# Block-sparse attention and a softplus layer on one core: the transposed probabilities written by one 128-row transpose and 16 copies by DMA instead of 16 small transposes

## The chip, the cores and the metric

The kernel runs on one core of one Trainium2 chip. The metric is device time in microseconds (us) of one launch, lower is better. Engines are named as in the profile: PE (TensorE matmul), PEld (its weight loads), DVE (VectorE), ACT (ScalarE), POOL (GpSimd), and SP (SyncE), which here only issues DMAs. Each engine runs its own queue in order and waits on semaphores.

## The reference, cut to what matters

```python
# q, k, v: (8, 8, 576, 64); heads 0..3 local, heads 4..7 strided, stride 32
scores = scale * np.matmul(q, k.transpose(0, 1, 3, 2))
rel = pos[:, None] - pos[None, :]
mask_local = (rel >= 0) & (rel < 32)
mask_strided = (rel >= 0) & (pos[None, :] % 32 == pos[:, None] % 32)
attn = softmax(np.where(mask, scores, -1e9))
x = np.matmul(attn, v)            # -> (4608, 512)
h = x @ w_in                      # (4608, 2048)
g = np.maximum(h, 0.0) + np.log1p(np.exp(-np.abs(h)))
out = g @ w_out                   # (4608, 512), float32
```

## The kernel before

**Attention.** The eight heads of a batch are handled as four pairs, so there are 32 pairs, numbered n = 0 to 31. A query sees at most 32 keys, so a block of 32 queries needs only 64 keys. For one pair the scores are a tile of 128 rows (two places times two heads times 32 queries) by 9 chunks of 64 keys. `head_scores` (L402 on PE) makes them, `add_mask` (L461), `row_maxima` (L466), `row_subtract` (L470), `row_exp` (ACT), `row_sums` (L493), `reciprocals` (L501) and `normalize` (L505) turn them into probabilities on DVE, in a tile of 128 by 576.

**Transposes.** The product with v needs the probabilities with keys in the partitions: a tile `pt` of 128 keys, for two heads, six key tiles `a` and three query blocks `i` of 32. Query block `i` has values only in the partition quarters `i` and `i + 1`; the other quarters stay zero. `prob_transposes` (L516) writes it straight: 16 transposes of 32 rows for a pair, eight of 192 columns and eight of 96, each moving its 32-row blocks to the quarter where they belong. In the planner they are four tasks of four instructions, `P{n}.0` to `P{n}`. `weighted` (L584 on PE) then multiplies with v. Except for a few pairs PE does the scores of pair n and the product of pair n - 1 in one stretch (`work` in `scores_of`); the text calls this the joint stretch.

**The layer.** The 4608 tokens are nine chunks of 512. `hidden` (L718) multiplies by w_in, `log_part` and `softplus` (L742) follow, `g_high` and `g_low` (L772) split the result in two parts, and `output` (L787) multiplies by w_out. Each product is three float32r products of high and low parts. The last four chunks are done two and two: seven products (`product`, L890) serve two chunks, with the sums of x and w made beforehand. One turn of that loop (a lap) has the products 1, 2, 5, 6, 3, 7, 4. The results are kept in four half tiles, `kept_0` and `kept_1`: ACT copies the bank of product 6 to the second half of `kept_1` (L981), product 7 then adds to the same bank, DVE joins product 3 to `kept_1` (L986), softplus writes the value back there, and SP stores it to DRAM as `far_u` (L748). The next lap's copy of product 6 may overwrite that half only when the store has landed.

**Order.** The first part of the program follows a list of names written out by hand (`FIRST`), up to pair 7. All later work is placed by `Plan`: each task has an urgency, an engine, a cost, what it waits for, and a lateness after its end for DMAs. The planner gives each task the first gap on its engine that is long enough, and the program's order on every engine is that of the planned start times. The planned times decide the order alone; on the chip each engine waits for what it really needs.

**DMA.** All DMAs of this part are issued by SP. They take eight semaphores in turn, so a DMA's issue also waits until the DMA eight places ahead has landed. A pair's q is loaded into the buffer of its probabilities (L284), its k into one of two buffers `kT` (L309), and v into one buffer (L320, L327). Weights w_in that no longer fit are streamed (L701), and in the laps SP loads `ws` (L969), `near` (L972) and `away` (L975).

The lines that fix the waits around the change:

```python
add(f"Y{n}{j}", y + j, "DVE", 0.47, fn, [f"S{n}", f"P{n-2}"])   # mask of pair n: its buffer is free
s2_free = [f"{spent}.{f-1}"] if f else s1_free                   # spent is the store of far_u
task("k2", "ACT", 0.6, fn, [f"P6.{A}.{f}", *s2_free])            # copy of product 6
mul("7", [f"k2.{A}.{f}"] + ([] if f else [...]))                 # product 7 adds to the same bank
```

## Time and profile before

| | |
|---|---|
| median of 3 runs | 864.98 us (863.56 to 865.66) |
| profiled execution, its own time | 865.16 us |
| its span (first to last instruction) | 863.1 us |
| granted PE clock | 1.0 throughout |
| ACT busy | 492.2 us (57%) |
| DMA: packets, bytes | 74477 packets, 119.49 MB, mean 138 GB/s |

The time of a run is some 2 us more than the span, for what lies around the first and last instruction. A busy share says little by itself: an engine may be busy all the time and still not set the end, and an engine with 74% may hold up another in one place. So the stretches and the waits are read, not the shares alone.

In the timeline a row has the start in us from the span's start, the time of the group, the engine, the line of the kernel, the operation with its tiles, and how many instructions were merged. A bracket at the end tells how long the engine was idle before it and what ended that. `SPq` rows are DMA issues: the time that SP spends on issuing, not the transfer.

### The profile page before, as it was taken

How to read it: one execution, taken by the hardware profiler on the slowest of the kernel's cores; microseconds unless marked ns; L12 is line 12 of the kernel's file. 1: busy time of each engine (PE TensorE's matmuls, PEld its weight loads, DVE VectorE, ACT ScalarE, POOL GpSimd, SP SyncE). 2: the span in 40 equal slices, each digit the busy share in tenths (PEclk: the TensorE clock that was granted, in tenths of full speed). 3: DMA queues.
4: the chain of work that ended last, by engine and by line, in shares of the span. 5: the costliest groups of instructions: out<-in, count | busy, mean ns of one | idle time of the engine just before them, and what ended most of it. 6: DMA issues, size and time to landing. Idle time of an engine off the chain costs nothing.

```text
span 863.1 us, 16559 instructions
## 1 busy us (share of the span) xinstructions
PE 853.4 (99%) x6536; PEld 700.7 (81%) x6536; DVE 640.9 (74%) x1370; ACT 492.2 (57%) x913; POOL 65.9 (8%) x88
## 2 busy tenths in 40 slices
PE   7999999999999999999999999999999999999998
PEld 6787888888888888888888888888888888888886
DVE  7899977898798879888788976677687746656500
ACT  6898755655555555546555555766664355566400
POOL 6345550000000000000000000000000000000000
PEclk9999999999999999999999999999999999999999
DMA  9794114646313453135424433655546143333100
GB/s 330 284 348 155 55 42 152 205 148 218 119 46 99 132 185 106 58 107 164 126 86 145 142 106 118 202 176 169 175 147 197 50 158 134 111 124 120 47 27 24
DMA packets 74477, 119.49 MB, mean 138 GB/s; under 512 B 5664, under 2 KB 41632, under 8 KB 74400
## 3 DMA queue, kind: packets, MB, share of 16 engines
q1 hardware_dynamic: 74112, 118.12, 41.4%
q8 instruction: 51, 0.84, 0.4%
q10 hardware_dynamic: 288, 0.33, 0.1%
q14 instruction: 26, 0.21, 0.1%
HBM read 88.01 MB, written 30.41 MB: 137 GB/s over the span
## 4 chain that ended last, share of the span: by engine, by line
PE 92%; DVE 4%; ACT 2%; issue 1%; DMA 0%; POOL 0%; ACTq 0%; POOLq 0%
PE py L787 43%; PE ph L718 23%; PE bank_a L890 10%; PE bank_c L890 5%; PE bank_b L890 2%; PE pv L584 2%; PE ps L402 2%; PE po L584 2%; PE py_last L787 1%; PE po L402 1%; PE pt L554 1%; DVE home L516 1%; DVE a_i L672 0%; DVE a_o L672 0%; DMA raw_q<-in_qk_dram 0%
## 5 line engine op out<-in xcount | busy, mean ns | idle before, releaser
L787 PE MATMUL py<-w_o,gh 128*128 128x512 f32 x1024 | 318.5, 392 | 0.0
L787 PEld LDWEIGHTS py<-w_o,gh 128*128 128x128 f32 x1024 | 190.3, 188 | 41.4 <-DVE o L287 0.3
L718 PE MATMUL ph<-x_h,w_i 128*128 128x512 f32 x656 | 202.8, 390 | 0.5 <-DVE u L742 0.5
L787 PE MATMUL py<-w_o,gl 128*128 128x512 f32 x512 | 199.3, 389 | 0.0
L516 DVE STREAM_TRANSPOSE home<-home 32x192 f32<-32x192 f32 x448 | 140.7, 318 | 7.1
L718 PEld LDWEIGHTS ph<-x_h,w_i 128*128 128x128 f32 x656 | 122.6, 188 | 26.7 <-POOL home L505 0.9
L718 PE MATMUL ph<-x_l,w_i 128*128 128x512 f32 x328 | 127.7, 389 | 0.0
L287 ACT CAST gh<-u 128x512 fp32r<-128x512 f32 x89 | 55.2, 621 | 107.7 <-DVE u L742 84.7
L787 PEld LDWEIGHTS py<-w_o,gl 128*128 128x128 f32 x512 | 96.1, 188 | 20.3
L730 ACT ACTIVATE u<-ph 128x512 f32<-128x512 f32 x84 | 50.1, 598 | 90.8 <-PE ph L718 88.2
L772 DVE TENSOR_TENSOR gl<-u,gh 128x512 fp32r<-128x512 f32 x117 | 80.8, 691 | 19.3 <-ACT gh L287 15.7
L735 ACT ACTIVATE u<-u 128x512 f32<-128x512 f32 x144 | 90.9, 632 | 3.8
L733 ACT ACTIVATE u<-u 128x512 f32<-128x512 f32 x144 | 90.9, 632 | 3.6
L718 PEld LDWEIGHTS ph<-x_l,w_i 128*128 128x128 f32 x328 | 61.6, 188 | 13.0
L742 DVE SCALAR_TENSOR_TENSOR u<-ph,u 128x512 f32<-128x512 f32 x84 | 57.7, 687 | 13.7 <-ACT u L735 12.5
L730 ACT ACTIVATE u<-kept 128x512 f32<-128x512 f32 x45 | 28.4, 631 | 41.1 <-DVE kept L986 25.6
L287 DVE COPY o<-py 128x512 f32<-128x512 f32 (+1 forms) x15 | 10.0, 669 | 45.6 <-PE py L787 45.5
L986 DVE TENSOR_TENSOR kept<-bank_c,kept 128x512 f32<-128x512 f32 x15 | 10.4, 692 | 33.8 <-PE bank_c L890 33.8
L287 ACT COPY home<-home 128x576 f32<-128x576 f32 x26 | 33.4, 1284 | 1.7 <-DMA home<-in_qk_dram 1.7
L287 ACT COPY o<-py 128x512 f32<-128x512 f32 (+1 forms) x21 | 11.5, 574 | 38.4 <-PE py L787 27.6
L461 DVE TENSOR_TENSOR home<-ps,home 128x384 f32<-128x384 f32 x28 | 15.5, 554 | 23.5 <-PE ps L402 22.0
L981 ACT COPY kept<-bank_a 128x512 f32<-128x512 f32 x30 | 17.6, 586 | 25.8 <-PE bank_a L890 24.2
(197 smaller groups left out, 1188.7 us busy)
## 6 DMA issues: line engine op xcount, KB each, us to landing
home<-in_qk_dram SPq DMA_DIRECT2D x56, 288.0 KB, 3.2
ws<-far SPq DMA_DIRECT2D x30, 512.0 KB, 3.3
home<-in_v_dram SPq DMA_DIRECT2D x28, 320.0 KB, 3.8
out_dram<-o SPq DMA_DIRECT2D x35, 256.0 KB, 2.4
ri<-in_moe_w_in_dram SPq DMA_DIRECT2D x16, 512.0 KB, 7.4
ro<-in_moe_w_out_dram SPq DMA_DIRECT2D x16, 512.0 KB, 8.3
far_w<-w_i SPq DMA_DIRECT2D x16, 512.0 KB, 4.7
w_i<-far_w SPq DMA_DIRECT2D x16, 512.0 KB, 3.3
```

Of the source, the lines that this page charges most:

```text
L287: (engine.copy if engine is nc.scalar else engine.tensor_copy)(dst, src)
L402: nc.tensor.matmul(pss[n, part][to : to + 32, at : at + 64], lhsT=qT[head, c : c + 32], rhs=k_of(n)[head, c : c + 64], start=True, stop=True,)
L516: nc.vector.transpose(pt[32 * (i + c) : 32 * (i + c) + 32, h, a : a + hi - lo, 32 * i : 32 * i + 32,], src[:, lo:hi, 32 * c : 32 * c + 32],)
L584: nc.tensor.matmul(po[64 * h : 64 * h + 64, TILE * x : TILE * x + TILE], lhsT=vs[n][:, a, h, :], rhs=pt_of(n, a)[:, h, a % 2], start=True, ...
L718: nc.tensor.matmul(ph, lhsT=w_i(c, f)[:, half, cc * P : (cc + 1) * P], rhs=x_at(x, cc, c), start=(i == 0), stop=(i == 3 * NCC - 1),)
L730: nc.scalar.activation(us[c, f], phs[c, f], AF.Abs)
L733: nc.scalar.activation(u, u, AF.Exp, scale=-1.0)
L735: nc.scalar.activation(u, u, AF.Ln, bias=1.0)
L742: nc.vector.scalar_tensor_tensor(to, in0=ph, scalar=0.0, in1=u, op0=ALU.max, op1=ALU.add)
L772: engine.tensor_tensor(g, us.pop((c, f)), ghs[c, f].bitcast(F32), op=ALU.subtract)
L787: nc.tensor.matmul(y_of(c, t), lhsT=g[:, sl], rhs=w32["o", f][:, half], start=(f == ROWS[c][0] and n == 0), stop=(f == ROWS[c][-1] and n = ...
L890: nc.tensor.matmul(bank, lhsT=w_left(p, A, f, half, i), rhs=x_right(p, A, part, i), start=p in "125" and n == 0, stop=n == 5, skip_group_c ...
```

## The change

Pair 8 and the pairs before it keep the 16 transposes. From pair 9 on:

- `turn` transposes the whole tile of 128 by 576 in one DVE instruction into a tile `turned`. Each 32 by 32 block is transposed where it stands, so a block comes out in the quarter in which its queries were.
- `move` then copies the blocks to the quarters of `pt_late` where the keys belong, by 16 DMAs issued by SP: eight of 32 rows by 192 values (768 bytes a row), eight of 32 rows by 96 values (384 bytes a row).
- `pt_late` lies where `pt` lay, with the query blocks outermost, so that each copy has one run of bytes in a row. POOL clears the quarters that hold no values once, ahead of pair 8.
- `turned` takes the second k buffer, so from pair 10 on k has one buffer, and k of pair n + 1 is loaded after the scores of pair n.
- The buffer of the probabilities is free after `turn`, so the mask of pair n + 2 and q of pair n + 2 wait for that and not for the copies.
- In the planner a turn costs 0.8 us on DVE, a move 1.6 us on SP with 2.5 us of lateness.

```diff
+    pt_late = homes[0][:, : 2 * S].rearrange("p (h i a l) -> p h i a l", h=2, i=3, l=32)
+    turned = homes[2][:, PAD + S : PAD + 2 * S].rearrange("p (c x l) -> p c x l", c=2, l=32)
...
+    FAR_MOVES = 2 * NPAIR + 2
...
-        return kT_early[n] if n < NPAIR else kT[n % 2]
+        return kT_early[n] if n < NPAIR else kT[n % 2 if n < FAR_MOVES else 0]
...
+    def clear_late():
+        for i, spans in enumerate((((2, 2),), ((0, 1), (3, 1)), ((0, 2),))):
+            for q, n in spans:
+                nc.gpsimd.memset(pt_late[32 * q : 32 * (q + n), :, i], 0.0)
+
+    def turn(n):
+        nc.vector.transpose(turned, prob_of(n).rearrange("p x (c l) -> p c x l", l=32))
+
+    def move(n):
+        for part, (lo, hi) in enumerate(SPLIT):
+            for place in range(2):
+                a, i = block_at(lo, place)
+                for h in range(2):
+                    at = 64 * place + 32 * place_of(part, h)
+                    for c in range(2):
+                        nc.sync.dma_start(
+                            pt_late[32 * (i + c) : 32 * (i + c) + 32, h, i, a : a + hi - lo],
+                            turned[at : at + 32, c, lo:hi],
                         )
...
-                    rhs=pt_of(n, a)[:, h, a % 2],
+                    rhs=pt_of(n, a)[:, h, a % 2] if n < 2 * NPAIR else pt_late[:, h, :, a],
...
-            add(f"Y{n}{j}", y + j, "DVE", 0.47, fn, [f"S{n}", f"P{n-2}"])
+            free = f"T{n-2}" if n - 2 > 2 * NPAIR else f"P{n-2}"
+            add(f"Y{n}{j}", y + j, "DVE", 0.47, fn, [f"S{n}", free])
...
-        for j in range(4):
-            name = f"P{n}" if j == 3 else f"P{n}.{j}"
-            fn = lambda j=j: prob_transposes(n, (j,))
-            add(name, y + 8.5 + 1.3 * j, "DVE", 1.25, fn, after)
-            after = [name]
+        if n == 2 * NPAIR:
+            add("clear", 0.0, "POOL", 3.0, clear_late)
...
+        else:
+            read = f"T{n}"
+            add(read, y + 8.5, "DVE", 0.8, lambda: turn(n), after + [f"P{n-1}"])
+            add(f"P{n}", y + 9.5, "SP", 1.6, lambda: move(n), [read], 2.5)
+        nk = n + (1 if n >= FAR_MOVES else 2)
+        if n != FAR_MOVES - 1 and nk < len(order):
+            add(f"k{nk}", x + 5, "SP", 0.8, lambda: load_k(nk), [f"S{n}"], 2.0)
         if n + 2 < len(order):
-            add(f"k{n+2}", x + 5, "SP", 0.8, lambda: load_k(n + 2), [f"S{n}"], 2.0)
-            add(f"q{n+2}", x + 18, "SP", 0.8, lambda: load_q(n + 2), [f"P{n}"], 2.0)
+            add(f"q{n+2}", x + 18, "SP", 0.8, lambda: load_q(n + 2), [read], 2.0)
```

The order on PE is the same as before, row by row. Three places show what moves on the other queues and in the waits.

DVE, in the second lap of the first two-chunk loop, around the transposes of pair 28 (`home_95` holds the probabilities, `home_94` is `pt`, `kept_1` the half tiles that are stored). Before, the end of the first twelve transposes and the last four:

```order
L516 STREAM_TRANSPOSE home_94<-home_95 32x6x32 x2
L516 STREAM_TRANSPOSE home_94<-home_95 32x3x32 x2
L742 SCALAR_TENSOR_TENSOR kept_1_6147<-kept_1_6147,u_1_6353 128x512
L986 TENSOR_TENSOR kept_1_6147<-bank_b_2_6410,kept_1_6147 128x512
L516 STREAM_TRANSPOSE home_94<-home_95 32x6x32 x2
L516 STREAM_TRANSPOSE home_94<-home_95 32x3x32 x2
```

After, where `home_96` holds `turned`:

```order
L509 TENSOR_TENSOR home_95<-home_95,st_6292 128x576
L535 STREAM_TRANSPOSE home_96<-home_95 128x576
L766 SCALAR_TENSOR_TENSOR kept_1_6169<-kept_1_6169,u_1_6375 128x512
L766 SCALAR_TENSOR_TENSOR kept_0_6190<-kept_0_6190,u_9_6405 128x512
L1010 TENSOR_TENSOR kept_1_6169<-bank_b_2_6443,kept_1_6169 128x512
```

Twelve small transposes stood between `normalize` and the softplus that makes the stored value; one large one stands there now.

SP, at the same place of the same lap (DMA issues). Before:

```order
L975 DMA away_6127<-far_w_2554 128x2x256
L972 DMA near_5898<-far_w_2066 128x1024
L748 DMA far_u_1_6434<-kept_1_6147 128x512
L284 DMA home_95<-in_qk_dram 128x576
L748 DMA far_u_9_6464<-kept_0_6168 128x512
L969 DMA ws_0_5392<-far_3_5737 128x1024
```

After:

```order
L999 DMA away_6149<-far_w_2567 128x2x256
L545 DMA home_94<-home_96 32x192 x8
L545 DMA home_94<-home_96 32x96 x8
L772 DMA far_u_1_6450<-kept_1_6169 128x512
L288 DMA home_95<-in_qk_dram 128x576
L772 DMA far_u_9_6460<-kept_0_6190 128x512
L996 DMA near_5938<-far_w_2070 128x1024
L993 DMA ws_0_5419<-far_3_5687 128x1024
```

The 16 copies stand ahead of both stores of the lap and of the load of `near`; the same holds in the laps of pairs 29 and 30.

PE, the product of pair 9 with v inside a joint stretch, with the semaphores that each row waits for. Before:

```order
L584 MATMUL po_2219<-home_94,home_95 64x96 [waits DMAHW2_49,DVE_49]
L584 MATMUL po_2219<-home_94,home_95 64x96 [waits DVE_49]
L584 MATMUL po_2219<-home_94,home_95 64x96 [waits DMAHW3_49]
L584 MATMUL po_2219<-home_94,home_95 64x96 x3
L584 MATMUL pv_2262<-home_94,home_95 64x96 [waits DVE_49]
```

After:

```order
L608 MATMUL po_2228<-home_94,home_95 64x96 [waits DMAHW4_49,DMAHW5_49,DMAHW1_49,DMAHW0_49]
L608 MATMUL po_2228<-home_94,home_95 64x96 [waits DMAHW6_49,DMAHW7_49,DMAHW3_49,DMAHW2_49]
L608 MATMUL po_2228<-home_94,home_95 64x96 x4
L608 MATMUL pv_2271<-home_94,home_95 64x96 [waits DMAHW1_49,DMAHW0_49,DVE_49]
L608 MATMUL pv_2271<-home_94,home_95 64x96 [waits DMAHW3_49,DMAHW2_49]
```

PE waited for DVE and two DMAs (v); now it waits for all eight DMA semaphores, and for more of them in one row.

More of the change, by code (lines that the diff above doesn't have):

```diff
@@ L515, in prob_transposes @@
                     for c in range(2):
-                        nc.vector.transpose(
-                            pt[
-                                32 * (i + c) : 32 * (i + c) + 32,
-                                h,
-                                a : a + hi - lo,
-                                32 * i : 32 * i + 32,
-                            ],
-                            src[:, lo:hi, 32 * c : 32 * c + 32],
+                        to = slice(32 * (i + c), 32 * (i + c) + 32)
+                        if n < 2 * NPAIR:
+                            dst = pt[to, h, a : a + hi - lo, 32 * i : 32 * i + 32]
+                        else:
+                            dst = pt_late[to, h, i, a : a + hi - lo]
+                        nc.vector.transpose(dst, src[:, lo:hi, 32 * c : 32 * c + 32])
+    def clear_late():
[14 more added lines that the diff above has]
+                            turned[at : at + 32, c, lo:hi],
                         )
@@ L1222, in scores_of @@
             after = [f"{letter}{n}"]
-        for j in range(4):
-            name = f"P{n}" if j == 3 else f"P{n}.{j}"
-            fn = lambda j=j: prob_transposes(n, (j,))
-            add(name, y + 8.5 + 1.3 * j, "DVE", 1.25, fn, after)
-            after = [name]
+        if n == 2 * NPAIR:
+            add("clear", 0.0, "POOL", 3.0, clear_late)
+            for j in range(4):
+                name = f"P{n}" if j == 3 else f"P{n}.{j}"
+                fn = lambda j=j: prob_transposes(n, (j,))
+                add(name, y + 8.5 + 1.3 * j, "DVE", 1.25, fn, after + ["clear"])
+                after = [name]
+            read = f"P{n}"
+        else:
+            read = f"T{n}"
[4 more added lines that the diff above has]
+            add(f"k{nk}", x + 5, "SP", 0.8, lambda: load_k(nk), [f"S{n}"], 2.0)
         if n + 2 < len(order):
-            add(f"k{n+2}", x + 5, "SP", 0.8, lambda: load_k(n + 2), [f"S{n}"], 2.0)
-            add(f"q{n+2}", x + 18, "SP", 0.8, lambda: load_q(n + 2), [f"P{n}"], 2.0)
+            add(f"q{n+2}", x + 18, "SP", 0.8, lambda: load_q(n + 2), [read], 2.0)
     def needs_of(n):
```

## The prediction

> **What bounds the kernel now.** I read the page first, then the busy time by stretch.
>
> ```profile
> span 863.1 us, 16559 instructions
> PE 853.4 (99%) x6536; PEld 700.7 (81%) x6536; DVE 640.9 (74%) x1370; ACT 492.2 (57%) x913; POOL 65.9 (8%) x88
> PE 92%; DVE 4%; ACT 2%; issue 1%; DMA 0%; POOL 0%; ACTq 0%; POOLq 0%
> ```
>
> ```profile
> 76.00:514.00 438.00, 438.00 (x3833) 359.64 (x3833) 370.57 (x854) 252.69 (x467) 30.13 (x28) 1.00 0.38 123
> 514.00:655.00 141.00, 140.89 (x945) 115.88 (x944) 100.15 (x194) 89.80 (x152) 0.00 (x0) 1.00 0.50 163
> 655.00:863.00 208.00, 204.56 (x919) 168.63 (x918) 103.46 (x181) 86.85 (x148) 0.00 (x0) 1.00 0.29 95
> ```
>
> The first fence has each engine's busy time and the chain of waits that ended last, which is PE for 92%. The second gives the length of a stretch, then the busy time of PE, PEld, DVE, ACT and POOL in it. From 76 to 655 us, where nearly all of the change takes effect, PE is idle for 0.1 us. What PE is idle in the whole span lies before 76 us, ahead of the change, and after 655 us (3.4 us), where the last results leave. PE's order and its matmuls do not change. So the change can take nothing off the path: whatever it saves on DVE falls beside a full PE. The time can stay or grow, and the question is only whether PE is made to wait in a place where it did not.
>
> **What DVE saves.**
>
> ```profile
> L516 DVE STREAM_TRANSPOSE home<-home 32x192 f32<-32x192 f32 x224 | 81.8, 365 | 3.3
> L516 DVE STREAM_TRANSPOSE home<-home 32x96 f32<-32x96 f32 x224 | 60.5, 270 | 3.8
> ```
>
> A pair's 16 transposes are 8 x 0.365 + 8 x 0.270 = 5.1 us. From 96 to 192 columns the price grows by 0.095 us, so one of 576 columns is 0.365 + 4 x 0.095 = 0.75 us by estimate. Over 23 pairs some 100 us of DVE's 640.9 go. On the path that is worth 0, by the windows above, at most the 0.1 us.
>
> **What SP gets.** 16 issues a pair. The trace has no copy from SBUF to SBUF, so the spacing s of the issues and the landing time L are bounded by the nearest rows: the first issues of the program, which follow each other without a wait, and stores (number, KB of each, median us from issue to landing).
>
> ```profile
> 0.73 0.40 SPq L284 DMA_DIRECT2D raw_q<-in_qk_dram  x1
> 1.18 0.42 SPq L309 DMA_DIRECT2D early_l<-in_qk_dram  x1
> 1.65 0.42 SPq L284 DMA_DIRECT2D raw_q<-in_qk_dram  x1
> 2.11 0.43 SPq L309 DMA_DIRECT2D early_l<-in_qk_dram  x1
> ```
>
> ```profile
> out_dram<-o SPq DMA_DIRECT2D x35, 256.0 KB, 2.4
> far_u<-kept SPq DMA_DIRECT2D x14, 256.0 KB, 3.6
> out_dram<-o SPq DMA_DIRECT2D x1, 128.0 KB, 1.7
> ```
>
> Back to back the spacing is 0.45 to 0.47 us. A single issue after a pause takes 0.32 us (near, below), and with the 0.05 us between two rows (1.18 + 0.42 to 1.65) that is s = 0.37. The new copies have a quarter of the rows, so I take s = 0.43 and keep 0.37 and 0.47. A move then holds SP for 16 x 0.43 = 6.9 us (5.9 to 7.5), where the planner reckons with 1.6. For the copies I take L = 2.4, between 1.7 and 4.8 (the slowest landing among the stores and loads of far_u, in the last fence). With L below 8 x 0.43 the ninth copy does not wait for the first one's semaphore.
>
> In a sentence apart: the Trainium skill, "DMA: Bandwidth & Descriptors", section "Issuing engines are not separate DMA queues", says that the sequencer's time to start a DMA is usually small relative to the DMA itself, and its section "Anatomy of one DMA" puts the dispatch at about 50 ns, for the path from GpSimd. By that a move would be 16 x 0.05 = 0.8 us by estimate, and the result that of rival 1; the issue rows here, 0.32 to 0.43 us, speak against it.
>
> **Pairs 9 to 27, the joint stretches.** The one at 245 us, DVE then PE:
>
> ```profile
> 234.37 0.76 DVE L505 TENSOR_TENSOR home<-home,st 128x576 f32<-128x576 f32 x1
> 235.16 2.64 DVE L516 STREAM_TRANSPOSE home<-home 32x192 f32<-32x192 f32 x8
> 239.92 2.58 DVE L516 STREAM_TRANSPOSE home<-home 32x192 f32<-32x192 f32 x8
> ```
>
> ```profile
> 245.72 0.72 PE L584 MATMUL po<-home,home 128*64 128x96 f32 x12
> 246.27 0.67 PE L584 MATMUL pv<-home,home 128*64 128x96 f32 x12
> ```
>
> Before, the last transpose ends at 242.50 and PE reads at 245.72. Now the turn ends at 235.16 + 0.75 = 235.91, the copies are issued from 235.95, the twelfth at 235.95 + 11 x 0.43 = 240.7, the last at 242.4. The first half of the product (po) needs the first twelve, landed at 243.1, so 2.6 us to spare; the second (pv) needs all, landed at 244.8, 1.5 us to spare. So 0 here, and the cover, PE's rows of the layer, is 1.5 us longer than the move. If it goes, each of the 18 joint stretches from 170 to 490 us pays the excess (rival 2).
>
> What stands behind a move on SP is late by up to 6.9 us: q of pair n + 2 (needed a whole pair later), the streamed weights and stores of weights. For a stream:
>
> ```profile
> 407.62 0.32 SPq L701 DMA_DIRECT2D w_i<-far_w  x1
> ```
>
> ```profile
> 402.61 1.32 DVE L516 STREAM_TRANSPOSE home<-home 32x192 f32<-32x192 f32 x4
> ```
>
> ```profile
> w_i<-far_w SPq DMA_DIRECT2D x16, 512.0 KB, 3.3
> ```
>
> ```profile
> 418.10 2.72 PE ph L718 x12
> ```
>
> The load issued at 407.62 is for the row of hidden that starts at 418.10; landing in 3.3 us it has 7.2 us left. The move of that pair starts at 402.61 + 0.75 = 403.4 and ends at 410.3, so the load goes out 3 us later and is still covered by PE's rows in between: 0; without that cover the excess would fall on PE once for each stream. Pairs are (402.61 - 235.16) / 9 = 18.6 us apart, so a k that is loaded one pair ahead instead of two still has most of that: 0. POOL, busy for 30 of the 438 us, clears `pt_late` once beside PE's rows: 0.
>
> **Waits on PE.** The product now waits for eight DMA semaphores, which gives five more wait instructions for each pair in the built program.
>
> ```profile
> L584 PEldq EVENT_SEMAPHORE  x27: 51/51/51, 23.3 to 666.0; - x27
> ```
>
> Exposed they would cost 5 x 0.051 x 23 = 5.9 us. In the stretch from 76 to 514 us such instructions stand already and PE is not idle for any of it: I take 0 and keep 0 to 5.9.
>
> **Pairs 28 to 30, in the laps.** Here the move stands ahead of a store on which PE's path hangs:
>
> ```profile
> 561.50 0.75 DVE L505 TENSOR_TENSOR home<-home,st 128x576 f32<-128x576 f32 x1
> 562.28 3.98 DVE L516 STREAM_TRANSPOSE home<-home 32x192 f32<-32x192 f32 x12
> 566.29 0.69 DVE L742 SCALAR_TENSOR_TENSOR kept<-kept,u 128x512 f32<-128x512 f32 x1
> ```
>
> ```profile
> 562.50 0.52 SPq L975 DMA_DIRECT2D away<-far_w  x1
> 566.58 0.32 SPq L972 DMA_DIRECT2D near<-far_w  x1
> 567.01 0.35 SPq L748 DMA_DIRECT2D far_u<-kept  x1
> ```
>
> ```profile
> 571.21 0.59 ACT L981 COPY kept<-bank_a 128x512 f32<-128x512 f32 x1 [0.29 <-DMA far_u<-kept]
> ```
>
> ```profile
> 572.50 1.07 PE L890 MATMUL bank_a<-t,ws 128*128 128x512 f32 x4
> ```
>
> The bracket carries the argument: already before, ACT's copy of product 6 starts when the store of far_u lands. It ends at 571.80, and product 7, which adds to the same bank, starts at 572.50. That store has 0.70 us to spare, no more.
>
> Now: the turn ends at 562.28 + 0.75 = 563.03, with the issue of away over at 563.02. The move runs from 563.05 to 563.05 + 6.9 = 569.93. The store's value is ready earlier than before, since twelve transposes no longer stand ahead of it on DVE, but its issue stands behind the move: 569.93 instead of 567.01. It lands 3.6 us later (the group's median), the copy starts 0.08 behind, takes 0.59, and product 7 starts at 569.93 + 3.6 + 0.67 = 574.2 instead of 572.50: PE waits 1.7 us. The loads behind (near) have until the next lap.
>
> The two other laps have the same distances:
>
> ```profile
> 594.55 3.98 DVE L516 STREAM_TRANSPOSE home<-home 32x192 f32<-32x192 f32 x12
> ```
>
> ```profile
> 604.77 1.52 PE L890 MATMUL bank_a<-t,ws 128*128 128x512 f32 x6
> ```
>
> ```profile
> 626.84 3.98 DVE L516 STREAM_TRANSPOSE home<-home 32x192 f32<-32x192 f32 x12
> ```
>
> ```profile
> 637.05 1.29 PE L890 MATMUL bank_a<-t,ws 128*128 128x512 f32 x5
> ```
>
> From the first transpose to product 7 it is 10.2 us in all three. So 3 x 1.7 = 5.1 us. With s = 0.37 and a landing of 2.0 the wait is below 0, so 0; with s = 0.47 and 4.8 it is 563.05 + 7.5 + 4.8 + 0.67 - 572.50 = 3.5, times three 10.6. For pair 31 the product itself is the next that PE needs:
>
> ```profile
> 656.17 1.31 DVE L516 STREAM_TRANSPOSE home<-home 32x192 f32<-32x192 f32 x4
> ```
>
> ```profile
> 670.10 0.39 PE L584 MATMUL pv<-home,home 128*64 128x96 f32 x4
> ```
>
> The turn would end at 656.9, the move at 663.8, the last copy land at 665.8: 4 us to spare, 0. The slowest landing that bounds L:
>
> ```profile
> DMA to landing us min/median/max: 2.0/3.1/4.8
> ```
>
> **Sum.** The profiled execution took 865.16 us, 2.1 more than its span, and is 0.2 above the median of the runs. 865.2 + 0 (DVE) + 0 (joint stretches) + 0 (wait instructions) + 5.1 (laps) = 870.3.
>
> **Rivals.**
> 1. *Not slower: the store still lands in time.* Same place, the laps. It decides at 16 s + L = 572.50 - 563.05 - 0.67 = 8.8 us: with s = 0.37 a landing of 2.9 is enough. For it: the copies are small, issues after a pause take 0.32, and the store no longer goes out just behind the 512 KB load of near. Against it: the back-to-back rows. Time 865.2, up to 867 with what is left of the wait. Chance 0.27.
> 2. *The copies land late and the joint stretches wait.* It decides at s = 0.43 with L over 3.9. With 4.8 each pays 0.9 us, 18 x 0.9 = 16, with the laps 886. For it: half of the copies have rows of 384 bytes. The Trainium skill, "DMA: Bandwidth & Descriptors", says in "Specifications" that below 512 B a DMA does read-modify-write, and in "Why small descriptors are slow (HBM only)" that transfers within SBUF do not suffer; no row here shows either. Against it: 24 KB instead of 256, and no HBM. Chance 0.07.
> 3. *Faster.* Only by waits that the windows do not show, such as matmuls that run slower beside a busy DVE. Chance 0.04; about 862.
>
> That the change does not do what it says is no rival: the order shows 345 transposes fewer.
>
> **How the numbers follow.** The forecast, a wait in the three laps, gets 0.62: 866.5 to 875.5, likeliest 870.3. The range of 864.6 to 876.0 takes in rival 1 and the laps with both bounds, and leaves out rivals 2 and 3. A measurement of this kernel can tell about 0.3% (2.6 us) from no change. Slower by more: 0.58 of the forecast and rival 2 make 0.65; same 0.31; faster 0.04.
>
> **What would show it.** DVE's busy time near 540 us. PE idle in the stretches up to 514 us as before, in the laps some 5 us, each in front of product 7, behind ACT's copy, behind the landing of far_u. 16 SP rows of some 0.4 us for each pair. I am wrong if the laps show no idle PE (s or L smaller), or if PE waits at the product with v in the joint stretches (L larger).

## The result, and the profile after

The changed kernel takes 907.12 us (median of 4 runs, 905.15 to 907.84), the kernel before 864.48 us beside it (863.56 to 865.66): a ratio of 1.0489, 95% interval 1.0466 to 1.0511. It is 42.6 us slower. The forecast was 870.3 us with a range up to 876.0; the direction was right, the size was not.

The page of the changed kernel, its span, the engines' busy time and the chain of waits that ended last:

```profile
span 905.8 us, 16805 instructions
PE 870.6 (96%) x6536; PEld 710.3 (78%) x6536; DVE 542.3 (60%) x1025; ACT 492.4 (54%) x913; POOL 67.5 (7%) x92
PE 67%; SPq 12%; DVE 8%; DMA 6%; ACT 4%; issue 3%; POOL 0%; DVEq 0%; ACTq 0%; POOLq 0%
```

DVE fell by 98.6 us, as reckoned, and that was worth nothing. PE now has 67% of the chain instead of 92%, and SP's issues, which had no share, have 12%. Where PE stands idle, by stretches (length, then the busy time of PE, PEld, DVE, ACT, POOL, then the granted clock, the DMA share and GB/s):

```profile
76.00:150.00 74.00, 74.00 (x583) 60.62 (x583) 63.21 (x141) 46.52 (x106) 31.71 (x32) 1.00 0.26 87
150.00:520.00 370.00, 356.95 (x3156) 290.99 (x3155) 219.57 (x417) 198.41 (x345) 0.00 (x0) 0.99 0.43 135
520.00:690.00 170.00, 157.82 (x1007) 127.54 (x1006) 90.50 (x155) 92.32 (x158) 0.00 (x0) 0.97 0.46 149
```

PE is full up to 150 us, as before. Then it is idle for 13.1 us in the part with the joint stretches (forecast: nothing) and for 12.2 us in the laps (forecast: some 5). The clock is below 1.00 in both, which it was nowhere before. What PE waits for (us in total, times, longest):

```profile
PE bank_a L914 <- ACT kept L1005: 11.8, 3, 4.1
PE pv L608 <- DMA home<-home: 10.9, 11, 2.4
```

The first is the wait that the forecast named, product 7 behind the copy of product 6, three times, but 4.1, 3.6 and 4.1 us long instead of 1.7. The second is the product with v waiting for the copies, which the forecast had priced at 0.

**The move on SP.** The group of all copies (duration ns min/median/max), one move in the timeline, and the landings (number, KB, median us):

```profile
L545 SPq DMA_DIRECT2D home<-home x368: 507/588/1556, 160.3 to 709.1; - x184
242.38 10.01 SPq L545 DMA_DIRECT2D home<-home  x16
home<-home SPq DMA_DIRECT2D x184, 24.0 KB, 1.8
home<-home SPq DMA_DIRECT2D x184, 12.0 KB, 1.8
```

A move holds SP for 10.0 us, 0.63 us for each copy, where the forecast took s = 0.43 and at most 0.47. The landing L is 1.8 us, for rows of 768 and of 384 bytes alike; it had been taken as 2.4.

**A joint stretch.** The turns of three pairs and the products of the first two:

```profile
241.57 0.78 DVE L535 STREAM_TRANSPOSE home<-home 128x576 f32<-128x576 f32 x1
261.04 0.78 DVE L535 STREAM_TRANSPOSE home<-home 128x576 f32<-128x576 f32 x1
280.39 0.78 DVE L535 STREAM_TRANSPOSE home<-home 128x576 f32<-128x576 f32 x1
```

```profile
252.31 0.84 PE L608 MATMUL po<-home,home 128*64 128x96 f32 x11
253.68 0.68 PE L608 MATMUL pv<-home,home 128*64 128x96 f32 x10 [0.42 <-DMA home<-home]
271.88 0.83 PE L608 MATMUL po<-home,home 128*64 128x96 f32 x11
274.55 0.87 PE L608 MATMUL pv<-home,home 128*64 128x96 f32 x10 [1.72 <-DMA home<-home]
```

The first half of the product (po) still finds its copies; the second (pv) waits for the last ones, 0.42 us here and 1.72 us at the next pair. The turns are 19.5 and 19.4 us apart, where a pair had 18.6 us: scores, softmax, turn, 10 us of issues, landing and product follow each other and take longer than PE's own work of a pair.

**A lap.** The turn and the move of pair 29, the store, the copy of product 6 and product 7:

```profile
587.02 0.78 DVE L535 STREAM_TRANSPOSE home<-home 128x576 f32<-128x576 f32 x1
```

```profile
587.86 10.64 SPq L545 DMA_DIRECT2D home<-home  x16
598.60 0.53 SPq L772 DMA_DIRECT2D far_u<-kept  x1
```

```profile
600.90 0.58 ACT L1005 COPY kept<-bank_a 128x512 f32<-128x512 f32 x1 [6.42 <-DMA far_u<-kept]
```

```profile
601.54 2.07 PE L914 MATMUL bank_a<-t,ws 128*128 128x512 f32 x6 [4.13 <-ACT kept L1005]
```

The chain is the one that the prediction drew, row for row: turn, move, store behind the move, landing 2.3 us later, copy, product 7. Only its longest link is 10.64 us instead of 6.9.

**A clock that halves.** Windows of 3.41 us of the changed kernel, with the columns as above (the last three are the granted clock, the DMA share and GB/s):

```profile
210.05:213.46 3.41, 1.37 (x54) 1.05 (x38) 2.00 (x5) 1.77 (x5) 0.00 (x0) 1.00 0.36 99
213.46:216.87 3.41, 3.01 (x15) 2.44 (x16) 1.29 (x4) 1.76 (x4) 0.00 (x0) 0.50 0.97 343
216.87:220.29 3.42, 3.42 (x16) 2.82 (x15) 3.22 (x7) 1.17 (x2) 0.00 (x0) 1.00 0.85 301
```

```profile
599.17:602.58 3.41, 1.04 (x5) 0.86 (x6) 0.69 (x1) 1.65 (x3) 0.00 (x0) 1.00 0.85 276
602.58:605.99 3.41, 3.41 (x10) 2.63 (x9) 3.00 (x5) 2.44 (x5) 0.00 (x0) 0.50 0.97 347
```

Behind a window in which PE worked for 1.37 or 1.04 us of 3.41 stands one at half clock: in the lap it holds 10 matmuls, where the window at full clock above holds 16 (in the first of the two, ten of the 15 are small ones of the product). There are five such windows, two in the joint stretches and one in each of the three laps, with 3.0, 3.4, 3.4, 3.4 and 3.1 us of busy PE. "PE busy" in them is a matmul at half speed, so this loss stands in no column of idle time.

**The account.** PE has the same instructions in the same order in both kernels, so the distances between the starts of successive matmuls can be subtracted one by one, changed kernel less the kernel without moves (below, `no_moves`, which takes as long as the one before). From 150 to 520 us of the latter PE falls 24.6 us behind: 19.8 at the product with v, 2.5 in `output` (behind it, at half clock) and 2.2 in `hidden` (1.2 of it behind one stream of weights that comes late). In the laps it falls 18.1 us behind: 14.7 at the products, 2.9 in `output`, 0.5 at the product with v. That is 42.7 us in all. The 19.8 us are spread unevenly: of the 18 joint stretches from 170 to 490 us eleven lose 0.4 to 3.4 us at the product, the other seven only some 0.2. They are more than the waits listed above (10.9 us at pv), because a wait is counted from the modelled end of the last matmul: one small matmul of the product lasts 0.246 us by itself, while twelve in a row take 0.72, so some 0.2 us of each wait passes as busy time.

### The profile page after: what moved, and what is told of

It is laid out like the page before. It is cut to its first block, busy times and chain, and to the rows that moved or that the text cites. A ratio compares the mean times of both kernels' runs of the same rounds, so it can differ in the third digit from the quotient of the medians.

```text
span 905.8 us, 16805 instructions
## 1 busy us (share of the span) xinstructions
PE 870.6 (96%) x6536; PEld 710.3 (78%) x6536; DVE 542.3 (60%) x1025; ACT 492.4 (54%) x913; POOL 67.5 (7%) x92
## 4 chain that ended last, share of the span: by engine, by line
PE 67%; SPq 12%; DVE 8%; DMA 6%; ACT 4%; issue 3%; POOL 0%; DVEq 0%; ACTq 0%; POOLq 0%
PE py L811 32%; PE ph L742 15%; SPq L545 11%; PE bank_a L914 8%; PE bank_c L914 4%; DMA home<-in_qk_dram 2%; PE pv L608 2%; PE bank_b L914 2%; DMA home<-home 1%; PE py_last L811 1%; PE po L608 1%; PE ps L406 1%; DVE home L535 1%; DVE u L766 1%; DMA far_u<-kept 1%
## 5 line engine op out<-in xcount | busy, mean ns | idle before, releaser
L811 PE MATMUL py<-w_o,gh 128*128 128x512 f32 x1024 | 322.1, 396 | 0.0
L811 PEld LDWEIGHTS py<-w_o,gh 128*128 128x128 f32 x1024 | 193.2, 191 | 42.6 <-issue 0.4
L291 ACT COPY home<-home 128x576 f32<-128x576 f32 x26 | 33.1, 1272 | 16.3 <-DMA home<-in_qk_dram 16.3
L914 PE MATMUL bank_a<-t,ws 128*128 128x512 f32 x90 | 25.7, 425 | 11.8 <-ACT kept L1005 11.8
L608 PE MATMUL pv<-home,home 128*64 128x96 f32 x372 | 26.4, 254 | 11.0 <-DMA home<-home 10.9
```

The source lines that it names most:

```text
L291: (engine.copy if engine is nc.scalar else engine.tensor_copy)(dst, src)
L608: nc.tensor.matmul(po[64 * h : 64 * h + 64, TILE * x : TILE * x + TILE], lhsT=vs[n][:, a, h, :], rhs=pt_of(n, a)[:, h, a % 2] if n < 2 * N ...
L811: nc.tensor.matmul(y_of(c, t), lhsT=g[:, sl], rhs=w32["o", f][:, half], start=(f == ROWS[c][0] and n == 0), stop=(f == ROWS[c][-1] and n = ...
L914: nc.tensor.matmul(bank, lhsT=w_left(p, A, f, half, i), rhs=x_right(p, A, part, i), start=p in "125" and n == 0, stop=n == 5, skip_group_c ...
```

## The experiments

The theory after this reading: SP's 10 us for each move are the cause, through what waits behind them. Rivals: the single k buffer and the new layout have a part in it; the laps are only late because the first part is; it is 16 copies and their semaphores wherever they are issued, and not the queue; q behind the move and not the product's copies sets the pace. Diffs are against the changed kernel. All kernels ran beside the kernel before, which took 863.5 to 864.5 us (medians).

**1. No moves** (`no_moves`): all pairs keep their 16 transposes, written into `pt_late`; one k buffer and the cleared tile stay.

```diff
-        if n == 2 * NPAIR:
-            add("clear", 0.0, "POOL", 3.0, clear_late)
+        if not MOVED(n):                # MOVED(n): False
+            if n == 2 * NPAIR:
+                add("clear", 0.0, "POOL", 3.0, clear_late)
             for j in range(4):
```

> The changed kernel with no turn and no move at all: every pair keeps its 16 transposes, written into the new layout; one buffer for the keys and the cleared tile stay. If only the moves cost: as before, 864 to 866. If the single buffer of the keys or the new layout has a part in it: over 867.

864.12 us, ratio 1.000 (0.9991 to 1.001). The single k buffer, the layout, the clearing and the wider stride of the product's operand cost nothing. All of the loss is in the turn and the moves.

**2. Moves in one part only** (`near_only`, `laps_only`): the same edit, with `MOVED` true for pairs 9 to 27, or for pairs 28 to 31.

> Turn and move for pairs 9 to 27 only; pairs 28 to 31 (the laps) go back to their 16 transposes, written into the new layout. If the laps and the joint stretches each pay on their own: the changed kernel's 907.1 less the some 18.3 us that PE falls behind in the laps, so about 889 (886 to 892), with PE idle in front of the product with v up to 520 us as in the changed kernel, none in front of product 7 and no half-clock window after 520 us. If the laps are late only because the first part has left the queues behind: still about 907.

> The opposite: pairs 9 to 27 keep their 16 transposes, pairs 28 to 31 are turned and moved. If the parts are independent: 864.5 plus some 18.3, so about 883 (880 to 886), PE full up to 514 us, and three waits of some 4 us in front of product 7, each with a window of half clock behind it. If the laps only wait as forecast (1.7 us each) without the first part: about 870.

891.19 us (1.0318, 1.0296 to 1.0341) and 881.81 us (1.0201, 1.0186 to 1.0216). The two losses are 26.7 and 17.3 us, together 44.0 where the whole change has 42.6. The parts are independent: the laps are late by themselves, with the first part as before.

**3. The store ahead of the move** (`store_first`): in the laps the planner's move also waits for the store, so that SP's order is store, q, store, near, move. The order on the other engines stays.

```diff
-            add(f"P{n}", y + 9.5, "SP", 1.6, lambda: move(n), [read], 2.5)
+            lap = 2 * (n - len(order) + NPAIR) + 1
+            after = [read] + [f"Us{NEAR+1}.{lap}"] * (lap > 0)
+            add(f"P{n}", y + 9.5, "SP", 1.6, lambda: move(n), after, 2.5)
```

> The changed kernel with one order changed on SP: in the laps the store of far_u goes out ahead of the move, all else stays. If the laps wait for nothing but that store: the loss of the laps goes, 907.1 - 17.3 = 890 (887 to 893), no PE idle in front of product 7 and no half clock after 520 us. If 10 us of SP per lap are too much wherever they stand (the loads of near, ws and away then come late): 897 or more.

892.22 us (1.0337, 1.0310 to 1.0365). The store, the move and the stretch of the laps in its profile:

```profile
588.33 0.32 SPq L772 DMA_DIRECT2D far_u<-kept  x1
...
591.61 0.57 SPq L545 DMA_DIRECT2D home<-home  x1
```

```profile
520.00:690.00 170.00, 169.31 (x1083) 138.66 (x1082) 102.39 (x175) 101.64 (x175) 0.00 (x0) 1.00 0.52 167
```

PE is idle for 0.7 us instead of 12.2, and the clock is back at 1.00. The laps waited for that store and for nothing else: the same move, a few rows later on the same queue, costs them nothing but wait instructions.

**4. Copies that nobody reads** (`idle_copies`, `in_place`): all pairs keep their 16 transposes, which the product reads; beside them SP issues 16 copies of the move's sizes at the move's place. In the first form they copy from the probabilities, in the second each turned block is written onto itself.

```diff
+            if n > 2 * NPAIR:           # in_place
+                add(f"T{n}", y + 8.5, "DVE", 0.8, lambda: turn(n), after + [f"I{n-1}"])
+                after = [f"T{n}"]
+                add(f"I{n}", y + 9.5, "SP", 1.6, lambda: idle_copies(n), after, 2.5)
             for j in range(4):          # the 16 transposes, as before
```

> All pairs keep their 16 transposes, and the product reads what they write; beside them SP issues, for pairs 9 to 31 and at the place of the move, 16 copies of the same sizes into a place that nobody reads. PE then waits for no copy. If it is SP's time that costs: the laps pay as in the changed kernel (the store of far_u stands behind 10 us of issues), some 18, and the joint stretches nothing but late streams, some 2: about 885 (880 to 890). If it is the product's own wait for its copies and PE's wait instructions that cost everywhere, in the laps too: 865 to 867.

> The copies that nobody reads once more, without the flaw of the first form, whose copies read the tile that the next load of q overwrites: the product reads the result of 16 transposes; beside them each pair is turned, and 16 copies of the move's sizes write the turned blocks onto themselves. If SP's time costs by itself: the laps pay as in the changed kernel (17 to 18), and up to 520 us only what is late behind 10 us of issues on SP (2 to 5): 882 to 890. If the cost sits in PE's wait for the copies: 865 to 868.

933.01 us (1.0808, 1.0781 to 1.0834) and 937.90 us (1.0849, 1.0820 to 1.0877): both expectations missed, by some 50 us and on the same side. I had put the first down to its copies reading the tile that q overwrites; the second has no such flaw and is no better. The waits of `in_place` name the reason (engine, line, what it waits for, us in total, times, longest):

```profile
ACT home L294 <- DMA home<-in_qk_dram: 59.0, 17, 8.8
```

In the changed kernel ACT waits 16.3 us for q in all, here 59.0. q of pair n + 2 stands behind the 16 copies of pair n on SP, and ACT's lay-out of q stands ahead of the exponential of the next pair and of the layer's activations. With the product no longer waiting, PE runs into the layer's late results instead: row by row, PE loses 27.7 us in `hidden` up to 520 us, 7.3 at the product and 8.8 in `output`. So 10 us on SP are dear even when nobody needs the copies, but the experiment had two causes in it.

**5. The same with q ahead of the copies** (`in_place_q_first`): transposes, turn, load of q, then the copies in place. The diff is against `in_place`. As the copies come some 6 us later by that, in the laps the loads of near and the first store of far_u stand ahead of them too.

```diff
-                add(f"T{n}", y + 8.5, "DVE", 0.8, lambda: turn(n), after + [f"I{n-1}"])
-                after = [f"T{n}"]
-                add(f"I{n}", y + 9.5, "SP", 1.6, lambda: idle_copies(n), after, 2.5)
+                add(f"T{n}", y + 13.8, "DVE", 0.8, lambda: turn(n), [f"P{n}", f"I{n-1}"])
+                if n + 2 < len(order):
+                    add(f"q{n+2}", y + 13.9, "none", 0.0, lambda: load_q(n + 2), [f"T{n}"], 2.8)
+                add(f"I{n}", y + 14, "SP", 1.6, lambda: idle_copies(n), [f"T{n}"], 2.5)
...
-        if n + 2 < len(order):
+        if n + 2 < len(order) and not 2 * NPAIR < n:   # q's old place
```

> The copies that nobody reads once more (16 transposes for the product, 16 copies in place beside them), with q's load ahead of them: the transposes, the turn, q, then the copies. If the loss of that form (938) came only from q standing behind the copies and from the store of far_u standing behind them: 865 to 872, with PE full up to 514 us. If 10 us of SP for each pair cost wherever they stand: 880 or more.

883.73 us (1.0227, 1.0210 to 1.0245). What PE waits for now:

```profile
PE ph L754 <- DMA w_i<-far_w: 9.5, 5, 4.6
```

54 us of the loss went with the order on SP: up to 520 us, where only q's place and the copies' 6 us can matter, 43.8 became 14.8, in the laps 26.9 became 3.8. It did not fall to 865 to 872: 14.5 us are still lost in `hidden`, where streams of weights come up to 4.6 us late behind the copies. The same number of issues costs 19 or 74 us by what stands behind them; each user of SP that stands behind 10 us of issues pays when its own cover is shorter.

**6. q ahead of the move in the changed kernel** (`q_first`; `q_and_store_first` has the edit of 3 as well). The order on ACT, DVE and PE stays.

```diff
+            if n + 2 < len(order):
+                add(f"q{n+2}", y + 9.5, "none", 0.0, lambda: load_q(n + 2), [read], 4.4)
             add(f"P{n}", y + 9.5, "SP", 1.6, lambda: move(n), [read], 2.5)
...
-        if n + 2 < len(order):
+        if n + 2 < len(order) and not 2 * NPAIR < n:   # q's old place
```

> The changed kernel with the load of q(n+2) issued on SP ahead of the move of pair n instead of behind it; the order on ACT, DVE and PE stays. Two closed loops are suspected in pairs 9 to 27, both some 19.4 us long, where PE's own work of a pair is 18.6. If the loop through q binds (move, q behind it, q's landing, ACT's lay-out of q, ACT's exponential of the next pair behind that, its turn, its move): some 16 to 20 us go, 887 to 891. If the loop through the product binds (scores, softmax, turn, 10.1 us of issues, landing, product in the next joint stretch behind the next scores): the move starts 0.4 us later and nothing is gained, 905 to 910.

> q's load and, in the laps, the store of far_u ahead of the move. If the loop through q binds and the laps wait only for the store: 865 + 4 (wait instructions) = 869 to 873. If the product's own copies bind: as with the store alone, 890 to 895.

912.60 us (1.0559, 1.0533 to 1.0584) and 893.35 us (1.0334, 1.0319 to 1.0350). Two rows of `q_first`: ACT's lay-out of q (busy, mean ns, idle before it and what ended that), and PE's wait at the product:

```profile
L291 ACT COPY home<-home 128x576 f32<-128x576 f32 x26 | 33.2, 1276 | 1.3 <-DMA home<-in_qk_dram 1.3
```

```profile
PE pv L608 <- DMA home<-home: 14.4, 14, 2.1
```

ACT's wait for q falls from 16.3 to 1.3 us, and the time does not fall with it; it grows by 5.5 us, somewhat past the 905 to 910 of the second case. That the move starts later by q's issue in each pair is the likely reason; no run separates it. The changed kernel is paced by the product's own copies. That wait of ACT was covered.

**7. Eight copies** (`eight`): only the first six chunks' blocks go by copies; those of the last three are transposed straight to their places.

```diff
-        for part, (lo, hi) in enumerate(SPLIT):           # in move
+        for part, (lo, hi) in enumerate(SPLIT[:1]):
...
-            add(read, y + 8.5, "DVE", 0.8, lambda: turn(n), after + [f"P{n-1}"])
-            add(f"P{n}", y + 9.5, "SP", 1.6, lambda: move(n), [read], 2.5)
+            add(f"t{n}", y + 8.5, "DVE", 0.8, lambda: turn(n), after + [f"P{n-1}"])
+            add(read, y + 9.4, "DVE", 2.2, lambda: prob_transposes(n, range(4), (1,)), [f"t{n}"])
+            add(f"P{n}", y + 9.5, "SP", 1.6, lambda: move(n), [f"t{n}"], 2.5)
```

> A move of 8 copies: the last three chunks' blocks are transposed straight to their places as before (8 x 0.27 us on DVE), only the first six chunks' go by copies, 8 x 0.633 = 5.1 us on SP. If it is a matter of how late the last copy is (5.1 + 1.8 us behind the turn, some 3 us ahead of the product): the joint stretches pay only the wait instructions (some 0.2 each, 4 in all) and the laps up to 0.4 each: 867 to 872. If each copy costs its share wherever it stands: half of the loss, 886.

871.33 us (1.0082, 1.0067 to 1.0097): half of the copies, a sixth of the loss. The joint stretch near 246 us, of `eight` and then of `no_moves`, from the first product to the first row of `output`:

```profile
246.00 0.84 PE L609 MATMUL po<-home,home 128*64 128x96 f32 x11
247.35 0.73 PE L812 MATMUL py<-w_o,gh 128*128 128x512 f32 x2
```

```profile
245.12 0.72 PE L611 MATMUL po<-home,home 128*64 128x96 f32 x12
246.26 0.73 PE L814 MATMUL py<-w_o,gh 128*128 128x512 f32 x2
```

1.35 us against 1.14: 0.21 us more, though no row waits for a DMA. It is 0.18 to 0.23 us in nearly all 21 stretches, 4.3 us in all. Most of the rest is one row of `hidden` that starts 1.9 us late at 478.8 us, behind DVE's `x_l`: DVE had stood for 5.5 us until a store of weights landed, which SP had issued behind the copies. The wait instructions at that line (duration ns min/median/max), in the changed kernel, in `eight` and in `two_queues`:

```profile
L608 PEldq EVENT_SEMAPHORE  x146: 51/51/1162, 23.2 to 711.8; - x146
```

```profile
L609 PEldq EVENT_SEMAPHORE  x100: 51/51/51, 22.7 to 672.2; - x100
```

```profile
L609 PEldq EVENT_SEMAPHORE  x192: 51/51/382, 20.8 to 677.2; - x192
```

Before there were 27. `eight` has 73 more, three for each pair, which at 0.051 us are 3.7 us, near the 4.3 lost. But 0.051 us for each is no rule: the changed kernel has five more for each pair and loses the same 0.18 us in the stretches in which it waits for no copy.

**8. The same 16 copies on two queues** (`two_queues`): ten on SP, six on POOL's queue.

```diff
-                        nc.sync.dma_start(
+                        k = 8 * part + 4 * place + 2 * h + c
+                        (nc.gpsimd if k % 8 in (2, 5, 7) else nc.sync).dma_start(
```

> The changed kernel with all its 16 copies, ten of them issued on SP (6.3 us) and six on POOL's queue (some 6 us at 1.0 us each), which stands idle there. If only the time on one queue counts: the last copy lands some 8.5 us behind the turn instead of 12, the joint stretches pay the wait instructions alone (some 0.2 to 0.3 each, 5 in all), the laps up to 1.1 each, now and then a stream is late (2): 869 to 876. If 16 copies or their semaphores cost wherever they are issued: 885 or more.

873.74 us (1.0119, 1.0102 to 1.0136). It is 10.3 us slower than the kernel before beside it: some 32 of the 42.6 us are gone with the copies all still there, so it is the time on one queue. The joint stretches pay 0.42 us each, row by row, with 165 wait instructions more than before, seven for each pair (8.4 us at 0.051), so more semaphores cost more; the laps pay 1.0, 0.1 and 0.4 us at product 7.

**9. What an issue costs** (`issue_kinds`): bursts of 16 DMAs of one kind.

> No part of the computation: bursts of 16 DMAs each, of one kind per burst. On SP: 128 and 32 rows of 768 B from DRAM to SBUF, 32 rows to DRAM, 32 rows of 768 and of 384 B and 128 rows of 768 B within SBUF; then 32 rows within SBUF on ACT's queue and on POOL's. If the number of rows sets the issue: the three bursts of 32 rows alike, and less than the ones of 128. If SBUF at both ends sets it: the bursts within SBUF at 0.63 us each whatever the rows, the ones with DRAM at one end at 0.43 to 0.47.

The bursts on SP, ACT's and POOL's queue, first issue to the end of the last (POOL's two rows are two of its 16 each):

```profile
39.93 7.40 SPq L39 DMA_DIRECT2D d<-in_x_dram  x16
47.44 7.32 SPq L39 DMA_DIRECT2D far<-src  x16
62.42 10.54 SPq L39 DMA_DIRECT2D c<-src  x16
76.32 10.00 SPq L39 DMA_DIRECT2D c32h<-src  x16
89.66 10.18 SPq L39 DMA_DIRECT2D c<-src  x16
103.38 10.16 ACTq L39 DMA_DIRECT2D a<-src  x16
119.31 1.05 POOL L39 DMA_DIRECT2D p<-src  x2 [0.99 <-issue]
121.30 1.06 POOL L39 DMA_DIRECT2D p<-src  x2 [0.94 <-issue]
```

In this order: 32 rows of 768 B from DRAM, the same to DRAM, then within SBUF 32 rows of 768 B, 32 of 384 B, 128 of 768 B, and 32 of 768 B on ACT's queue. With DRAM at one end an issue of 32 rows takes 0.46 us, within SBUF 0.63 to 0.66, whatever the rows and the bytes, on ACT's queue as on SP's. The burst of 128 rows from DRAM, ahead of these, has 0.47 to 0.48 from its eighth issue on; its first seven, beside a store of 1536 KB that was still on its way, take up to 1.3. The rows, on which the forecast had argued, do next to nothing. On POOL two take 2.0 us from row to row (119.31 to 121.30), so 1.0 us each.

**10. When the clock halves** (`stalls`, `stalls_small`): dense matmuls with PE stalls between them; in the second the joint stretch's small matmuls stand around each stall.

```diff
+    for cols in [1] + COLS + COLS[::-1]:
+        for _ in range(110):
+            nc.tensor.matmul(acc, lhsT=rhs[:, :P], rhs=rhs, start=True, stop=True)
+        nc.vector.tensor_copy(seen[:, :1], acc[:, :1])
+        nc.vector.memset(spare[:, :cols], 0.0)      # the length of the stall
+        nc.vector.memset(rhs[:, :4], 0.5)
```

> No part of the computation: dense matmuls of 128 x 512 in stretches of some 23 us, and between them PE waits for a chain of three DVE operations of growing length, once upwards and once downwards. If the half-clock windows behind the stalls of the changed kernel come from the stalls' length: stalls of up to 1 us leave the clock at 1.00, those of 2.5 us and more are each followed by a window of 3.4 us at 0.50, and between lies the bound, which depends on where in the 3.413 us grid a stall falls (1.9 us was enough at one place in the changed kernel, 1.97 not at another). If they come from something else: no window at any length.

> No part of the computation: the dense stretches of the test of stalls again, with the joint stretch's small matmuls around the stall, 48 of 64 x 32 x 64 ahead of it and 12 of 128 x 64 x 96 behind it. If a half-clock window comes when too little of 3.4 us is real matmul work, small matmuls counting little: windows already behind stalls of 1.7 to 2.6 us, which left the clock at 1.00 between dense stretches (the bound there lay between 2.80 and 3.33). If only PE's idle time counts: none below 2.8 us here either.

A stall is given here as the idle time of PE ahead of the next matmul; the expectations count from the start of the last matmul, which is 0.4 us more in `stalls` and 0.2 in `stalls_small`. In `stalls` all stalls of up to 2.42 us left the clock alone, and all of 2.95 us and more were followed by half clock; the expectation had the bound too low. In `stalls_small` one stall of 1.87 us and one of 2.93 us were followed by it; the other of 1.87, the other of 2.93, both of 2.4 and both of 2.1 us were not. Windows laid, to within 0.1 us, on the grid of 3.41 us in which the clock changes, of `stalls` and of `stalls_small` (length, then PE, PEld, DVE, POOL; the last three numbers are again clock, DMA share and GB/s):

```profile
125.84:129.25 3.41, 1.52 (x8) 0.53 (x7) 1.51 (x3) 0.00 (x0) 1.00 0.00 0
129.25:132.67 3.42, 3.42 (x17) 1.54 (x16) 0.00 (x0) 0.00 (x0) 1.00 0.00 0
177.04:180.45 3.41, 1.34 (x7) 0.39 (x4) 1.54 (x2) 0.00 (x0) 1.00 0.00 0
180.45:183.87 3.42, 2.53 (x7) 0.89 (x7) 0.82 (x2) 0.00 (x0) 0.51 0.00 0
```

```profile
157.16:160.58 3.42, 1.55 (x56) 0.95 (x55) 1.66 (x4) 0.00 (x0) 0.99 0.02 5
160.58:163.99 3.41, 3.41 (x20) 1.44 (x20) 0.00 (x0) 0.00 (x0) 0.51 0.00 0
269.78:273.19 3.41, 1.85 (x53) 1.05 (x51) 1.19 (x3) 0.00 (x0) 1.00 0.01 2
273.19:276.61 3.42, 2.04 (x20) 1.10 (x21) 1.32 (x2) 0.00 (x0) 1.00 0.00 0
```

What counts is how little PE does within one window of a fixed grid, not the length of the stall. 1.34 us of dense work were too little and 1.52 enough; 1.55 us, most of them with small matmuls, were too little as well. A stall of 2.93 us that the grid cut in two (1.85 and 2.04 us busy) did nothing; one of 1.87 us in a single window, next to small matmuls, did. The windows on the grid of all kernels here agree: with dense work alone, every one with up to 1.4 us of busy PE was followed by half clock and none with 1.5 or more; with small matmuls in it, the changed kernel's at 271.5 us was with 1.69 us, and in `q_first` one with 1.8 us at 349.2 was and one with 1.7 us at 509.6 was not. That is how a stall in a joint stretch can halve the clock: the scores and the product are small matmuls already. The exact weight of a small matmul was not measured and stays open. The Trainium skill, "TensorE: Matmul & The Clock Gate", section "Part 1: The HAM clock gate", says that the clock is set by a free-running window of 3413 ns; the grid of the windows here agrees. Its section "Why this matters for your kernels" advises against gaps of more than about 3 us between bursts of matmuls; the gap that halved the clock here was shorter, 1.87 us.

## Why the prediction was right in direction and wrong in size

- **DVE's saving, 0:** right. DVE has 98.6 us less to do, and nothing of it shows; `no_moves`, with all of DVE's work, is as fast as the kernel before.
- **The spacing s, 0.43 with bounds 0.37 and 0.47:** wrong, and this is the step on which the rest fell. It is 0.63. The bounds came from rows with DRAM at one end, and the choice within them from the smaller number of rows; `issue_kinds` shows that the two ends in SBUF make the difference and the rows next to none. In the Trainium skill, "DMA: Bandwidth & Descriptors", section "Issuing engines are not separate DMA queues", the time of an issue counts as usually small relative to the DMA. Here one issue takes 0.63 us where the copy lands 1.8 us behind its issue, a third of that, and 16 of them in a row hold SP for 10 us; the trace does not agree.
- **The landing L, 2.4:** on the safe side. 1.8, for both sizes of row.
- **Joint stretches, 0:** wrong, for s alone. With s = 0.633 and L = 1.8 the prediction's own rows give the last copy at 235.95 + 15 x 0.633 + 1.8 = 247.2 where pv starts at 246.27: 0.9 us late, 18 times, 17 us. PE lost 19.8 us at the product, of which some 3.8 are wait instructions (21 x 0.18), so 16. That the two sums come so close is in part luck, since only eleven of the 18 stretches waited, for 0.4 to 3.4 us. What rival 2 described came true, PE waiting in the joint stretches, but through the spacing and not through the landing.
- **Wait instructions on PE, 0 (bounds 0 to 5.9):** wrong, though within the bounds. They are exposed: 0.18 us or a little more for each pair, some 4 us in all, in `eight` with three more as in the changed kernel with five more. PE idle for 0.1 us, from which the prediction argued, did not mean that such instructions are hidden when more stand in a row.
- **Laps, 3 x 1.7:** right mechanism, right place, right rows; mis-sized. The waits are 4.1, 3.6 and 4.1 us. By the prediction's sum with the measured terms, 563.05 + 10.1 + 2.3 + 0.67 - 572.50 = 3.6. Two sizes were off and partly cancelled: the move took 10.1 us instead of 6.9, the store of the lap shown landed in 2.3 us instead of 3.6. `store_first` shows that the store's place behind the move is all of it.
- **Not foreseen: the half clock.** Five windows in which PE's matmuls run at half speed, 16.4 us of busy time in them, so some 8 us lost; they follow the stalls and go with them.
- **Streams, 0:** one came late, for 1.2 of the 2.2 us lost in `hidden`. The cover that the prediction quoted held for the others.
- **Rival 1**, not slower, needed 16 s + L below 8.8 us and had 10.1 + 2.3. **Rival 3**, faster, had nothing for it: PE's matmuls are no quicker beside a less busy DVE.

Summed anew: 16 for copies that land late, 4 for wait instructions, 12 for the three laps, 8 for the half clock and 2 in `hidden` are 42, against 42.6 measured. The split between half clock and waits is worked out from the rows and not from a run that has the one without the other.

No version here beats the kernel before. PE was full there; the best that a lighter DVE could give is the same time, and the copies add waits. The cheapest form with copies is `eight` with 7 us of loss.

## What to carry to other kernels

Price an issue by a row of the same kind, with the same memories at both ends, or measure it by itself before a queue is given 16 of them: a burst of DMAs is first of all time on the queue that issues it, and everything behind it in that queue is late by that time. Where one engine is full, unloading another buys nothing, and wait instructions put into the full engine's stream, and each stall long enough to halve its clock, are a cost of their own. The place in the queue can matter more than the work: the same move behind one store, instead of ahead of it, cost the laps next to nothing (0.8 us instead of 18.1).

## What the runs showed of the hardware that was not expected

- An issue on SP takes 0.46 to 0.48 us with DRAM at one end and 0.63 to 0.66 us with SBUF at both, with 32 rows or 128 (and, within SBUF, with 384 bytes or 768); on ACT, measured within SBUF alone, 0.64; on POOL some 1.0 us.
- Copies within SBUF of 384-byte rows land as fast as those of 768 (1.8 us).
- The clock halves for a whole window of 3.41 us when PE was busy for some 1.4 us or less of the window ahead in dense work (1.52 us left it alone), and at up to 1.8 us with small matmuls in it.
- Wait instructions of 51 ns on PE's queue are not hidden by the matmuls around them where several stand together: three or five more at a product cost 0.18 us or a little more, seven more 0.39 to 0.55.
